# Separate logit products for the last batch's strided heads, ahead of its row products

## The chip, the cores and the metric

The kernel runs on one core of one Trainium2 chip. The metric is the device time of one execution in microseconds. Of the kernel before, three runs took 647.68, 648.56 and 649.07 us; their median is 648.56 us.

## The reference

Three stages follow each other. Attention has 4 batches, 8 heads, 576 positions and 64 features per head. Heads 0 to 3 ("local", kind 0) look at the last 32 positions, heads 4 to 7 ("strided", kind 1) at positions with the same remainder modulo 32. Its output, 2304 tokens by 512 features, goes to a mixture of 8 experts of which each token takes one, and then to a dense layer that takes the maximum of three products:

```
x = attn(q, k, v) -> (2304, 512)             # 4 local and 4 strided heads side by side
logits = (x / (|x| + 1e-6)) @ en.T / tau     # en: the 8 expert vectors, normalised
expert = argmax(logits); gate = softmax(logits)[expert]
y[t]   = gate[t] * (relu(x[t] @ w1[expert]) @ w2[expert])
out    = max(y @ w1', y @ w2', y @ w3') @ w_out
```

Token t is position t % 576 of batch t // 576. The kernel counts 18 tiles of 128 tokens; the last batch is given tiles 13 to 17, and tile 13 holds 64 tokens of batch 2 and 64 of batch 3.

## The kernel before, in words

The kernel writes its instructions in the order in which each engine is to carry them out; nothing reorders them later. So what stands behind an instruction on its engine waits when that instruction waits.

**Attention (attention, L696).** 44 groups of score blocks (11 a batch) go through a pipeline over the step number s: scores, maximum, exponential, norm, transposes, product with the values. The last of these, g_av (L421), copies its product with ScalarE into xT (L444), the attention output with features on partitions, 64 features of each of 2 heads on 128 partitions, two such halves c for each kind.

**Rows (tok_half, L458).** For tile i and one kind, two products (four for a tile with two batches) with xT as the weights and rhs_i as the moving operand turn the 128 tokens into rows. rhs_i has 136 columns: 128 of the identity, and 8 with the normalised expert vectors, so each row comes out with 128 features and 8 partial logits. A copy (ScalarE once the pipeline drains, L477) brings them from PSUM into rows; after kind 1, the row goes out to x_scr in HBM by a DMA on SyncE's queue (L482). The products' PSUM tiles have two buffers (ps_r).

**Routing of the last batch (route_stages(3), L491).** Its stages are carried out in this order (L648): logits, order, five squares, norm, gate, gate2. 
- logits (L508, VectorE): sums the four partial logits of each token (L511), then five short operations to the one-hot of the largest (L513 to L517).
- order (L585): TensorE counts the tokens of each expert (L590, L592), ranks the batch's tokens (rank, L525), adds up the token lists of tiles 0 to 12 (windows, L597 to L603) and runs a product that nobody reads (warm(WM), L604); VectorE works out slots and one-hots (L609 to L625, with the expert order eid_i at L624); windows of tiles 13 to 17 (L628); then the token lists win_i (L634 to L638).
- square (L502, ScalarE): the sum of squares of one tile's rows, both kinds.
- norm (L519, GpSimd): the root of the five sums by a power (L521), and an addition (L522). gate and gate2 make the softmax's weight from it.

**The first expert.** After the attention, gather(0) (L779, L997) fetches the first expert's rows from x_scr in three pieces by indirect DMAs, issued by GpSimd and addressed by win_i. SyncE loads the first weights (L130), after it has read eid_i (L626); from the third load on they stand behind a small GpSimd operation that waits for the last piece (L125). TensorE runs 6 products that nobody reads (L1005), then transposes the first two pieces (L815), runs 4 more such products (L813), transposes the third, and after a split by ScalarE and VectorE (L797, L798) the expert's products begin (L822); these fill TensorE from there on.

An example of the order that matters here: `return [(0, f) for f in (logits, order)] + sq + [(0, f) for f in (norm, gate, gate2)]` (L648) puts the squares behind everything that logits and order give to ScalarE, and the norm ahead of gather(0) on GpSimd.

Of the kernel before, what the change touches and what calls it, by code (L numbers as in the profile page):

```python
# [9 lines left out]
F32 = mybir.dt.float32  # L10
# [5 lines left out]
ALU = mybir.AluOpType  # L16
AX = mybir.AxisListType
PSUM = bass.MemoryType.PSUM

B, H, S, D = 4, 8, 576, 64  # L20
NT, DM, E, F, F2 = 2304, 512, 8, 1024, 768
# [18 lines left out]
AGF = 500  # L40
NCF = 2
MID = 0
WM = 1
WN = 6
WX = 4
NOW0 = 7000
# [22 lines left out]
def kernel(ctx, tc, a, out, x_scr, w_scr, u_scr, perm_scr, gate_scr, upto="all"):  # L69
    nc = tc.nc  # L70
# [215 lines left out]
    ps_s = actx.enter_context(tc.tile_pool(name="ps_s", bufs=PSS, space=PSUM))  # L286
    ps_t = actx.enter_context(tc.tile_pool(name="ps_t", bufs=PST, space=PSUM))
    ps_x = actx.enter_context(tc.tile_pool(name="ps_x", bufs=PSX, space=PSUM))
    ps_r = actx.enter_context(tc.tile_pool(name="ps_r", bufs=8 - PSS - PST - PSX, space=PSUM))
# [20 lines left out]
    rhs_i = pa.tile([128, 4, 136], F32, name="rhs_i")  # L310
    junk = pa.tile([128, 512], F32, name="junk")

    vv, xT = {}, {}
# [42 lines left out]
    later, later_v = [], []  # L356

    def flush(fs):
        while fs:
            fs.pop(0)()  # L360
# [89 lines left out]
    first_tile = {0: 0, 1: 4, 2: 9, 3: 13}  # L450
    n_tiles = {0: 4, 1: 5, 2: 4, 3: 5}
    rows = {}
# [2 lines left out]
    def bc(ap, shape):  # L455
        return ap.to_broadcast(shape)

    def tok_half(i, kind):  # L458
        ps = ps_r.tile([128, 512], F32, tag="r", name="r")
        psv = ps[:, 0:272].rearrange("p (c n) -> p c n", c=2)  # L460
        segs, done = [], 0
        while done < 128:
            b, off = divmod(128 * i + done, S)
            n = min(128 - done, S - off)
            segs.append((done, b, off, n))
            done += n
        for c in range(2):
            for p0, b, off, n in segs:
                nc.tensor.matmul(  # L469
                    out=psv[p0:p0 + n, c, :], lhsT=xT[b, kind][:, c, off:off + n],  # L470
                    rhs=rhs_i[:, 2 * kind + c, :], start=True, stop=True)
        bq = max(b for b in range(B) if i >= first_tile[b])
        if bq not in rows:
            rows[bq] = row_p.tile([128, 5, 4, 136], F32, tag="row", name="row")
        dst = rows[bq][:, i - first_tile[bq], 2 * kind:2 * kind + 2, :]
        if on_act[0]:
            later_v.append(lambda: nc.scalar.activation(out=dst, in_=psv, func=ACTF.Copy))  # L477
        else:
            later_v.append(lambda: nc.vector.tensor_copy(out=dst, in_=psv))
        if kind == 1:  # L480
            r = rows[bq][:, i - first_tile[bq], :, 0:128]
            later_v.append(lambda: nc.sync.dma_start(  # L482
                out=x_scr[128 * i:128 * i + 128, :].rearrange("n (c d) -> n c d", c=4), in_=r))

    def warm(n, what=cf, pool=None, tag="t"):

        ps = (pool or ps_t).tile([128, 512], F32, tag=tag, name="warm")
        for _ in range(n):
            nc.tensor.matmul(out=ps[:, 0:256], lhsT=what[:, 0:128], rhs=what[:, 0:256], start=True, stop=True)

    def route_stages(b):  # L491
# [4 lines left out]
        def small(nm, dt=F32):  # L496
            return sm_p.tile([128, 5, 1], dt, tag=nm, name=nm)[:, 0:T, :]

        def wide(nm, n=E, dt=F32):
            return sm_p.tile([128, 5, n], dt, tag=nm, name=nm)[:, 0:T, :]  # L500
# [7 lines left out]
        def logits():  # L508

            d["l"], d["mx"], v, vm = wide("l"), small("mx"), wide("v"), small("vm")  # L510
            nc.vector.tensor_reduce(  # L511
                out=d["l"], in_=rows[b][:, 0:T, :, 128:136].rearrange("p t c e -> p t e c"), axis=AX.X, op=ALU.add)
            nc.vector.tensor_reduce(out=d["mx"][:, :, 0], in_=d["l"], axis=AX.X, op=ALU.max)  # L513
            nc.vector.tensor_tensor(out=v, in0=d["l"], in1=bc(d["mx"], s8), op=ALU.is_ge)
            nc.vector.tensor_tensor(out=v, in0=v, in1=bc(edesc.unsqueeze(1), s8), op=ALU.mult)
            nc.vector.tensor_reduce(out=vm[:, :, 0], in_=v, axis=AX.X, op=ALU.max)
            nc.vector.tensor_tensor(out=oh_all[:, t0:t0 + T, :], in0=v, in1=bc(vm, s8), op=ALU.is_equal)  # L517
# [67 lines left out]
        def order():  # L585


            oh, ee = oh_all[:, t0:t0 + T, :], [128, E, E]
            ps = ps_s.tile([128, 512], F32, tag="s", name="cnt")[:, 0:E]
            nc.tensor.matmul(out=ps, lhsT=ones, rhs=coh, start=True, stop=False)  # L590
            for t in range(T):
                nc.tensor.matmul(out=ps, lhsT=ones, rhs=oh[:, t, :], start=False, stop=t == T - 1)  # L592
            rank()

            tb = ps_t.tile([128, 512], F32, tag="t", name="tb")[:, 0:NW]

            def windows(t):  # L597
                for u in range(2):
                    nc.tensor.matmul(
                        out=tb, lhsT=lo_oh[:, t, :], rhs=w_tok[:, t, u, :], start=t == u == 0, stop=t == NTILE - 1 and u == 1)  # L600

            for t in range(t0):
                windows(t)  # L603
            warm(WM)  # L604
            key, pos = (sm_p.tile([128, E], F32, tag=n, name=n) for n in ("key", "pos"))
            tmp = sm_p.tile(ee, F32, tag="tmp", name="tmp")
            sl, lo, w = wide("sl"), small("lo", I32), small("w", I32)
            z = z_all[:, t0:t0 + T]
            nc.vector.scalar_tensor_tensor(out=key, in0=ps, scalar=8.0, in1=edesc, op0=ALU.mult, op1=ALU.add)  # L609
            nc.vector.tensor_tensor(out=sl, in0=d["rkv"], in1=bc(ebase.unsqueeze(1), s8), op=ALU.add)  # L610
            nc.vector.tensor_tensor(out=cmp, in0=bc(key.unsqueeze(1), ee), in1=bc(key.unsqueeze(2), ee), op=ALU.is_gt)
            nc.vector.tensor_tensor(out=sl, in0=sl, in1=oh, op=ALU.mult)
            nc.vector.tensor_reduce(out=pos, in_=cmp, axis=AX.X, op=ALU.add)
            with nc.allow_low_precision(reason="whole numbers below 2**15"):
                nc.vector.tensor_reduce(out=z, in_=sl, axis=AX.X, op=ALU.add)
            nc.vector.tensor_tensor(
                out=posoh, in0=bc(pos.unsqueeze(1), ee), in1=bc(iota[:, 0:E].unsqueeze(2), ee), op=ALU.is_equal)
            nc.vector.tensor_scalar(out=lo[:, :, 0], in0=z, scalar1=127, scalar2=None, op0=ALU.bitwise_and)
            nc.vector.tensor_scalar(out=w[:, :, 0], in0=z, scalar1=7, scalar2=None, op0=ALU.arith_shift_right)
            nc.vector.tensor_tensor(out=tmp, in0=posoh, in1=bc(iota[:, 0:E].unsqueeze(1), ee), op=ALU.mult)  # L620
            d["lo"], d["w"] = lo, w
            onehots()
            with nc.allow_low_precision(reason="whole numbers below 8"):
                nc.vector.tensor_reduce(out=eid_i, in_=tmp, axis=AX.X, op=ALU.add)  # L624
            tokens()  # L625
            ev[0] = nc.sync.value_load(eid_i[0:1, 0:1], min_val=0, max_val=E - 1)  # L626
            w_load()
            for t in range(t0, NTILE):  # L628
                windows(t)

            for q0, q1 in ((0, 1), (1, E)):
                w4 = [128, q1 - q0, NWIN, E]
                wp = sm_p.tile(w4, F32, tag=f"wp{q0}", name="wp", bufs=1)
                nc.vector.tensor_tensor(  # L634
                    out=wp, in0=bc(tb.rearrange("p (e i) -> p i e", e=E).unsqueeze(1), w4),
                    in1=bc(posoh[:, q0:q1].unsqueeze(2), w4), op=ALU.mult)
                with nc.allow_low_precision(reason="whole numbers below 2**12"):
                    nc.vector.tensor_reduce(  # L638
                        out=win_i[:, NWIN * q0:NWIN * q1].rearrange("p (q i) -> p q i", i=NWIN), in_=wp, axis=AX.X, op=ALU.add)
            nc.vector.tensor_copy(out=cnt_f, in_=ps)  # L640
# [48 lines left out]
    def embed3():  # L689
# [3 lines left out]
        nc.vector.tensor_copy(out=rhs_i[:, :, 128:136], in_=ep[:, 0:32].rearrange("p (c e) -> p c e", e=8))  # L693
        nc.vector.tensor_copy(out=rhs_i[:, :, 0:128], in_=bc(ident.unsqueeze(1), [128, 4, 128]))

    def attention():  # L696
        loads = [(b, kind) for b in range(B) for kind in range(2)][1:]
        toks, todo = [], []
        last = [0]
        for s in range(NG + LA + 1):  # L700
# [17 lines left out]
            if 0 <= s - LA < NG:  # L718
                g_av(s - LA)
                b, k = divmod(s - LA, 11)  # L720
                if k in (4, 10):
                    ts = range(first_tile[b], first_tile[b] + n_tiles[b])
                    toks += [lambda: None] * (DT if s < NG - 6 else 0) + [lambda i=i, k=k: tok_half(i, k // 6) for i in ts]
                if k == 10:
                    toks.append(lambda b=b: todo.extend(route_stages(b)))
                if s >= NG:
                    flush(later)
# [652 lines left out]
```

## Time and profile before

| | |
|---|---|
| median of 3 runs | 648.56 us |
| profiled execution | 645.76 us |
| its span, first to last instruction | 644.0 us |
| TensorE busy | 612.5 us, 95% of the span |
| VectorE busy | 448.6 us, 70% |
| ScalarE busy | 337.4 us, 52% |
| GpSimd busy | 134.8 us, 21% |
| mean granted TensorE clock | 0.983 of full |

The profile is that of one execution; its times are microseconds from the span's start. PE is TensorE's matrix products, PEld its weight loads, DVE VectorE, ACT ScalarE, POOL GpSimd and SP SyncE (SPq is its queue). A float32 product stands as two records, with a weight load each. A busy TensorE is not one at its best, since the ends of products are modelled.

### The profile page before, as it was taken

The page shows a single profiled execution, that of the slowest core. Times are in us where ns is not written, and L with a number is a line of the kernel's source. Part 1 is how long each engine was busy: PE and PEld are TensorE (multiplying, and loading weights), DVE is VectorE, ACT ScalarE, POOL GpSimd, SP SyncE. Part 2 cuts the span into 40 slices and gives each one's busy share as a digit, 9 for nine tenths or more (in the row PEclk, how much of TensorE's full clock was granted, in tenths as well). Part 3 has the DMA queues.
Part 4 walks back from the last instruction along what each step waited for, and adds up shares of the span by engine and source line. Part 5 has one row for each costly group of instructions (what it writes and reads, how often), then busy time and mean ns, then how long its engine had stood idle before and what let it go on. Part 6 is the DMA issues. An engine that isn't in the chain of part 4 may idle for free.

```text
span 644.0 us, 11933 instructions
## 1 busy us (share of the span) xinstructions
PE 612.5 (95%) x4281; PEld 576.7 (90%) x4282; DVE 448.6 (70%) x1011; ACT 337.4 (52%) x909; POOL 134.8 (21%) x131
## 2 busy tenths in 40 slices
PE   7899998799989999999999799999999999999995
PEld 6788886599979999999999699988999988999984
DVE  6878988577689788978897788787344376335440
ACT  3678877455566666656664534536412246221242
POOL 5434433354313142322210000002100012000021
PEclk8999999799989999999999999999999999999998
DMA  8998761674879596876864778921177301367111
GB/s 234 295 247 216 220 177 52 194 241 165 276 255 337 191 325 238 295 292 210 285 234 148 275 286 321 345 96 66 59 268 268 125 17 66 133 250 264 57 49 53
DMA packets 44881, 130.81 MB, mean 203 GB/s; under 512 B 4633, under 2 KB 15513, under 8 KB 41457
## 3 DMA queue, kind: packets, MB, share of 16 engines
q1 hardware_dynamic: 41792, 120.50, 56.3%
q0 software_dynamic: 3024, 9.49, 4.0%
q8 instruction: 36, 0.59, 0.4%
q14 instruction: 29, 0.23, 0.1%
HBM read 97.73 MB, written 32.24 MB: 202 GB/s over the span
## 4 chain that ended last, share of the span: by engine, by line
PE 80%; DVE 8%; DMA 8%; issue 1%; ACT 1%; SPq 1%; POOL 0%; POOLq 0%; DVEq 0%; ACTq 0%
PE g L822 61%; PE q L822 10%; DMA qs<-qs 2%; PE s L376 2%; PE x L434 2%; PE r L469 2%; PE q L805 1%; DMA ks<-kts 1%; DMA stage<-w_scr 1%; DMA out<-r,perm_i 1%; PE t L415 1%; DMA em<-emb 1%; DVE pt L417 1%; DVE mx L383 1%; DVE w L171 1%
## 5 line engine op out<-in xcount | busy, mean ns | idle before, releaser
L822 PE MATMUL g<-xc,w 128*128 128x384 f32 x1134 | 200.3, 336 | 4.8 <-DVE hf L1105 3.8
L822 PEld LDWEIGHTS g<-xc,w 128*128 128x128 f32 x1134 | 197.8, 189 | 7.0 <-issue 4.1
L171 DVE TENSOR_TENSOR w<-stage,w 128x1024 fp32r<-128x1024 f32 x76 | 105.9, 1405 | 26.4 <-ACT w L166 25.0
L822 PE MATMUL g<-h,w 128*128 128x376 f32 (+7 forms) x768 | 112.8, 303 | 2.2 <-DVE h L842 2.2
L822 PEld LDWEIGHTS g<-h,w 128*128 128x128 f32 x768 | 105.6, 190 | 3.5 <-DVE h L842 2.9
L822 PE MATMUL g<-xw,w 128*128 128x376 f32 (+7 forms) x768 | 106.0, 298 | 0.5 <-ACT xw L797 0.3
L822 PEld LDWEIGHTS g<-xw,w 128*128 128x128 f32 x768 | 104.3, 189 | 0.9 <-ACT xw L797 0.6
L166 ACT ACTIVATE w<-stage 128x1024 fp32r<-128x1024 f32 x76 | 79.3, 1056 | 16.1 <-DMA stage<-w 15.4
L1171 POOL DMA_INDIRECT out<-r,perm_i x18 | 17.8, 991 | 284.4 <-ACT r L1170 202.0
L822 PE MATMUL q<-w,hs 128*128 128x512 f32 x324 | 74.9, 390 | 1.3 <-DVE hs L1159 1.3
L822 PEld LDWEIGHTS q<-w,hs 128*128 128x128 f32 x324 | 60.6, 188 | 14.8 <-DVE hs L1159 2.6
L395 ACT ACTIVATE p<-s,nb 128x96 f32<-128x96 f32 (+2 forms) x152 | 50.6, 346 | 21.5 <-DVE r L404 16.0
L239 POOL TENSOR_TENSOR f<-f,c 128x512 int32<-128x512 int32 x24 | 31.4, 1307 | 117.1 <-DVE f L237 80.1
L1107 DVE TENSOR_TENSOR tmp<-g,yt 128x384 f32<-128x384 f32 x36 | 20.0, 555 | 44.6 <-PE g L822 44.4
L1120 ACT ACTIVATE yt<-g 128x384 f32<-128x384 f32 x27 | 13.3, 491 | 71.0 <-PE g L822 50.9
L407 POOL TENSOR_TENSOR p<-p,ri 128x384 f32<-128x384 f32 (+3 forms) x44 | 35.9, 816 | 59.2 <-DVE ri L406 45.2
L841 ACT ACTIVATE h<-g 128x376 fp32r<-128x376 f32 (+7 forms) x64 | 25.8, 410 | 29.8 <-PE g L822 27.9
L960 DVE TENSOR_TENSOR xc<-yt,xc 128x384 fp32r<-128x384 f32 x42 | 21.4, 553 | 15.7 <-ACT xc L959 15.7
L856 ACT ACTIVATE yt<-g 128x376 f32<-128x376 f32 (+7 forms) x32 | 13.2, 413 | 36.1 <-PE g L822 35.1
L417 DVE COPY pt<-t 96x512 f32<-96x512 f32 (+3 forms) x44 | 25.5, 581 | 8.0 <-PE t L415 7.8
L786 POOL DMA_INDIRECT xg<-x_scr,win_i x22 | 26.1, 1186 | 23.3 <-PE q L936 10.2
L395 ACT ACTIVATION_READ_ACCUMULATOR p<-s,nb 128x1 f32 (+2 forms) x152 | 31.0, 204 | 0.0
(175 smaller groups left out, 789.1 us busy)
## 6 DMA issues: line engine op xcount, KB each, us to landing
stage<-w SPq DMA_DIRECT2D x64, 512.0 KB
c<-wm SPq DMA_DIRECT2D x24, 512.0 KB
w<-u_scr SPq DMA_DIRECT2D x12, 1024.0 KB
u_scr<-w SPq DMA_DIRECT2D x9, 1024.0 KB
w<-u_scr SPq DMA_DIRECT2D x12, 768.0 KB
u_scr<-w SPq DMA_DIRECT2D x9, 768.0 KB
w_scr<-f SPq DMA_DIRECT2D x24, 256.0 KB
stage<-w_scr SPq DMA_DIRECT2D x12, 512.0 KB
```

The source lines that it names most:

```text
L166: nc.scalar.activation(out=ws[i][:, 0, 0:m], in_=x, func=ACTF.Copy)
L171: nc.vector.tensor_tensor(out=ws[i][:, 1, 0:m], in0=x, in1=ws[i][:, 0, 0:m].bitcast(F32), op=ALU.subtract)
L239: nc.gpsimd.tensor_tensor(out=f, in0=f, in1=low, op=ALU.add)
L395: nc.scalar.activation(out=p[:nq, i, :nk], in_=st[g]["ps"][:nq, i * nk:(i + 1) * nk], func=ACTF.Exp, bias=st[g]["nb"][:nq, i:i + 1], scale ...
L407: nc.gpsimd.tensor_tensor(out=d["p"][:nq, 0:ns, :nk], in0=d["p"][:nq, 0:ns, :nk], in1=ri[:nq, 0:ns].to_broadcast([nq, ns, nk]), op=ALU.mult)
L417: nc.vector.tensor_copy(out=pts[:nk, 0:ns, :nq], in_=pt[:nk, 0:ns * nq].rearrange("p (s q) -> p s q", s=ns))
L786: nc.gpsimd.indirect_dma_start(out=t[i][:r], out_offset=None, in_=x_scr, in_offset=bass.IndirectOffsetOnAxis(ap=win_i[:r, NWIN * e + i:NWI ...
L822: nc.tensor.matmul(out=ps, lhsT=ws(i), rhs=xs(j), start=first and n == 0, stop=last and n == 2, skip_group_check=more)
L841: nc.scalar.activation(out=h[:, 0], in_=ps, func=ACTF.Relu)
L960: nc.vector.tensor_tensor(out=x[:, 1], in0=src[c], in1=x[:, 0].bitcast(F32), op=ALU.subtract)
L1107: nc.vector.tensor_tensor(out=tmps[i], in0=ps, in1=s, op=ALU.add)
L1171: nc.gpsimd.indirect_dma_start(out=out, out_offset=bass.IndirectOffsetOnAxis(ap=perm_i[:, col:col + 1], axis=0), in_=r, in_offset=None)
```

## The change

The last batch's partial logits of the strided heads no longer come from the rows. A new function multiplies xT of kind 1 with the 8 expert columns alone, for all five tiles, into one PSUM tile. VectorE sums the two partial logits of the local heads from the rows and adds that PSUM tile. The row products of kind 1 come behind: three tiles (LR) in logits, two in order, behind the windows of tiles 0 to 12, where warm(WM) stood. The routing stages themselves keep their order.

```
+    def logit_products():
+        ps_l.append(ps_s.tile([128, 512], F32, tag="s", name="lg")[:, 0:40].rearrange("p (t e) -> p t e", e=E))
+        for t in range(n_tiles[B - 1]):
+            for p0, b, off, n in segments(first_tile[B - 1] + t):
+                for c in range(2):
+                    nc.tensor.matmul(
+                        out=ps_l[0][p0:p0 + n, t, :], lhsT=xT[b, 1][:, c, off:off + n], rhs=rhs_i[:, 2 + c, 128:136],
+                        start=c == 0, stop=c == 1, skip_group_check=True)
...
         def logits():
             d["l"], d["mx"], v, vm = wide("l"), small("mx"), wide("v"), small("vm")
+            m = 2 if b == B - 1 else 4
             nc.vector.tensor_reduce(
-                out=d["l"], in_=rows[b][:, 0:T, :, 128:136].rearrange("p t c e -> p t e c"), axis=AX.X, op=ALU.add)
+                out=d["l"], in_=rows[b][:, 0:T, 0:m, 128:136].rearrange("p t c e -> p t e c"), axis=AX.X, op=ALU.add)
+            if b == B - 1:
+                nc.vector.tensor_tensor(out=d["l"], in0=ps_l[0], in1=d["l"], op=ALU.add)
+                some_tiles(LR)
...
             for t in range(t0):
                 windows(t)
-            warm(WM)
+            some_tiles(n_tiles[b])
...
+    def some_tiles(n):
+        while n and later_tiles:
+            tok_half(later_tiles.pop(0), 1)
+            flush(later_v)
+            n -= 1
...
-                if k in (4, 10):
+                if k == 10 and b == B - 1:
+                    toks += [lambda: logit_products(), lambda: flush_todo(todo), last_route]
+                    later_tiles.extend(range(first_tile[b], first_tile[b] + n_tiles[b]))
+                elif k in (4, 10):
```

flush(later_v) carries out the ScalarE copy of the tile and the DMA to x_scr at that place; last_route carries out all stages of route_stages(3) one after the other.

## Rows read from the trace of the kernel before

**Rows 1.** The page: span, TensorE's busy time, the chain's shares by engine.

```profile
span 644.0 us, 11933 instructions
...
PE 80%; DVE 8%; DMA 8%; issue 1%; ACT 1%; SPq 1%; POOL 0%; POOLq 0%; DVEq 0%; ACTq 0%
```

**Rows 2.** The chain, 103 to 131 us: start, us, engine, what, line.

```profile
111.45 0.42 ACT xt L444
...
111.92 3.13 PE r L469 x22
...
115.06 0.41 ACT row L477
...
115.50 0.45 DVE l L511
...
117.15 0.29 PE cnt L592 x5
...
120.31 0.43 PE tb L599 x10
...
121.75 4.54 DMA xg<-x_scr,win_i
...
126.42 1.22 PE g L815 x8
127.64 1.73 PE warm L489 x8
...
130.70 0.44 PE g L822
```

**Rows 3.** Timeline of GpSimd, 119 to 125 us; in brackets idle time before, and releaser.

```profile
119.17 1.38 POOL L521 TENSOR_TENSOR nrm<-ssq,ca 128x5 f32<-128x5 f32 x1 [9.16 <-ACT junk L505]
120.64 0.24 POOL L522 TENSOR_SCALAR nr<-nrm 128x5 f32<-128x5 f32 x1
121.75 1.23 POOL L786 DMA_INDIRECT xg<-x_scr,win_i  x1 [0.86 <-DVE wp L634]
123.28 0.96 POOL L786 DMA_INDIRECT xg<-x_scr,win_i  x1 [0.31 <-issue]
```

**Rows 4.** Timeline of ScalarE: the first of the five squares, and the last one's end.

```profile
115.36 0.62 ACT L505 ACTIVATE junk<-row 128x512 f32<-128x512 f32 x1
...
118.90 0.19 ACT L505 ACTIVATION_READ_ACCUMULATOR junk<-row 128x1 f32 x1
```

**Rows 5.** Timeline of TensorE: weight loads (PEld) and products of three kinds.

```profile
105.70 0.41 PEld L415 LDWEIGHTS t<-cf,p 126*126 126x126 f32 x4 [0.17 <-issue]
...
111.91 0.42 PEld L469 LDWEIGHTS r<-rhs_i,xt 128*64 128x64 f32 x6 [0.54 <-ACT xt L444]
...
112.52 2.30 PEld L469 LDWEIGHTS r<-rhs_i,xt 128*128 128x128 f32 x16 [0.18 <-issue]
...
117.46 0.85 PE L599 MATMUL tb<-w_tok,lo_oh 128*128 128x24 bf16 x26
```

**Rows 6.** Timeline of VectorE: the last operation of batch 2's routing.

```profile
113.53 0.17 DVE L581 TENSOR_TENSOR coh<-coh,ohs 128x8 bf16<-128x8 bf16 x1
```

**Rows 7.** Timeline of SyncE: the last batch's five stores.

```profile
113.05 3.41 SPq L482 DMA_DIRECT2D x_scr<-row  x5
```

**Rows 8.** Stretches: length, busy us and instructions by engine, granted clock (1.00 full), DMA share, GB/s.

```profile
116.00:117.00 1.00, 0.00 (x0) 0.00 (x0) 0.86 (x5) 0.94 (x4) 0.00 (x0) 1.00 1.03 288
...
118.00:119.00 1.00, 1.00 (x14) 0.63 (x10) 1.00 (x8) 0.97 (x4) 0.00 (x0) 0.50 0.68 193
...
123.00:124.00 1.00, 1.00 (x4) 0.82 (x3) 0.17 (x1) 0.00 (x0) 0.72 (x1) 0.52 1.03 422
...
127.00:128.00 1.00, 1.00 (x8) 0.95 (x8) 0.95 (x1) 0.00 (x0) 0.00 (x0) 1.00 0.40 160
```

**Rows 9.** Timeline of TensorE: unread products, and the second piece's transposes' loads.

```profile
120.58 4.50 PE L489 MATMUL warm<-cf 128*128 128x256 f32 x12
...
126.98 0.42 PEld L815 LDWEIGHTS g<-cf,xg 128*128 128x128 f32 x4 [0.17 <-DMA xg<-x_scr,win_i]
```

More of the change, by code (lines that the diff above doesn't have):

```diff
@@ L42 @@
 MID = 0
-WM = 1
+LR = 3
 WN = 6
@@ L456, in bc, with segments @@
         return ap.to_broadcast(shape)
-    def tok_half(i, kind):
-        ps = ps_r.tile([128, 512], F32, tag="r", name="r")
-        psv = ps[:, 0:272].rearrange("p (c n) -> p c n", c=2)
+    def segments(i):
         segs, done = [], 0
@@ L466, in tok_half @@
             done += n
+        return segs
+    ps_l = []
+    def logit_products():
[6 more added lines that the diff above has]
+                        start=c == 0, stop=c == 1, skip_group_check=True)
+    def tok_half(i, kind):
+        ps = ps_r.tile([128, 512], F32, tag="r", name="r")
+        psv = ps[:, 0:272].rearrange("p (c n) -> p c n", c=2)
+        segs = segments(i)
         for c in range(2):
@@ L694, in embed3, with flush_todo, last_route @@
         nc.vector.tensor_copy(out=rhs_i[:, :, 0:128], in_=bc(ident.unsqueeze(1), [128, 4, 128]))
+    later_tiles = []
+    def flush_todo(todo):
+        while todo:
+            todo.pop(0)[1]()
+    def last_route():
+        for _, f in route_stages(B - 1):
+            f()
+    def some_tiles(n):
[3 more added lines that the diff above has]
+            n -= 1
     def attention():
@@ L720, in attention @@
                 b, k = divmod(s - LA, 11)
-                if k in (4, 10):
+                if k == 10 and b == B - 1:
+                    toks += [lambda: logit_products(), lambda: flush_todo(todo), last_route]
+                    later_tiles.extend(range(first_tile[b], first_tile[b] + n_tiles[b]))
+                elif k in (4, 10):
                     ts = range(first_tile[b], first_tile[b] + n_tiles[b])
                     toks += [lambda: None] * (DT if s < NG - 6 else 0) + [lambda i=i, k=k: tok_half(i, k // 6) for i in ts]
-                if k == 10:
+                if k == 10 and b < B - 1:
                     toks.append(lambda b=b: todo.extend(route_stages(b)))
```

## The prediction, made before the changed kernel was run

> **What bounds the kernel now.** The page comes first: TensorE holds 80% of the chain that ended last, and the profiled execution's span is 644.0 us [rows 1]. The rest of the chain matters where TensorE has nothing to do, so I read next the chain around the end of the attention, where the change lies. There the reader sees a relay: the last copy of xT, 22 product records for the strided rows, the last row copy, the logits, the counts, the last windows, then the gather of the first expert's rows at 121.75, its landing, the transposes, eight records of unread products, and the expert's products from 130.70 [rows 2]. Behind 130.70 TensorE runs nearly without a gap, so a microsecond at the first gather or at the transposes is a microsecond of the whole.
>
> The chain names one releaser for each step. So the third view is GpSimd's own timeline: the gather stands there behind the norm, which began at 119.17, when ScalarE's last square had ended, and with its addition ended at 120.88; the gather follows at 121.75 with 0.86 of idle time [rows 3]. The norm is late by less than a microsecond of being what holds the gather. This side branch (row copies, squares, norm, gather) is not in the chain, and it is what the change touches.
>
> **The change part by part.** Times below are on the profiled execution's clock.
>
> *The products.* They replace nothing; the 24 records (12 products) are added. Four belong to batch 2's half of tile 13 and can run before xT is ready. Of the 20 others, four load 64 columns and 16 load 128, and each moves only 8 columns. No such product stands in the trace. Below: 26 bf16 products with 24 columns took 0.85, 0.033 each; above: the rows' own records took 3.13 for 22, 0.142 each [rows 2, 5]. I take the weight loads as the limit, since these shrink with nothing: 0.41 for four of 126 columns, so 0.103, and 0.42 for six of 64, so 0.07 [rows 5]. That is 16 x 0.103 + 4 x 0.07 = 1.93 from 111.92, plus some 0.15 until the last result is there: 114.0 (112.7 to 114.9 by the ends).
>
> *The logits.* VectorE has batch 2's routing until 113.70 [rows 6], so cheap products would not be used sooner anyway. The sum over the local halves reads half of what L511 read in 0.45; about 0.3, until 114.0. The added operation and the five that follow cost what the five cost now: from 115.50 + 0.45 to 117.15 is 1.2, 0.24 each [rows 2]. One-hots at 114.05 + 0.24 + 1.2 = 115.5, where they now come at 117.1.
>
> *Three row tiles ahead of the counts.* These are 8 + 4 + 4 = 16 records on TensorE, 16 x 0.142 = 2.3 from about 113.85, so 116.1 (115.0 if they run at 0.07 and 0.103). The counts stand behind them: 116.1 instead of 117.15, a gain of 1.05, and not the 1.6 that the one-hots gain. The two VectorE chains from the counts to win_i are unchanged, so win_i would be ready 1.05 earlier, and the gather could leave at 120.7.
>
> *Two row tiles behind the windows.* On TensorE they take the place of unread products and end before the one-hots for the last windows are there, so they cost TensorE nothing. But all that a tile issues moves with it: its ScalarE copy and its store. The counts, the rank and the windows took 117.15 to about 118.15; so the two tiles begin at 117.1, need 8 x 0.142 = 1.14, and the last copy (0.41) ends at 118.7. Now it ends at 115.47 [rows 2]. **This is the price.** The five squares stand behind that copy on ScalarE: they took from 115.36 to 119.09 [rows 4], and the norm began 3.70 behind the last copy's end. It will begin at 122.4 and, with the same 1.71 to the end of the addition, end at 124.1. The gather stands behind it on GpSimd. With the 0.05 to 0.31 that separate waiting GpSimd operations [rows 3], it leaves at about 124.25 instead of 121.75: **+2.5**. Its bounds: with every TensorE record at its cheapest and the one-hots at 115.3, the last copy still ends at 117.5, which makes +1.35; with products at 0.142 and the clock halved while tiles 16 and 17 run, it ends near 120.2, which makes +4.0. That win_i is earlier is lost behind this.
>
> *SyncE's queue.* The two late stores stand there ahead of the reading of the first expert's number and the weight loads. Five stores took 3.41 to issue [rows 7], so two take 1.4, until about 119.9. The weights are not in the chain between the gather and 130.70 [rows 2], and they stay out of it when the gather is later. Costed at nothing; if they were late, it could be at most the 1 us or so by which their loads slip. gate and gate2 wait for the norm on VectorE, with weight splits behind them; these too have until the third transposes.
>
> *The clock.* The granted clock fell to half when TensorE had nothing to do from about 115.0 to 117.15, and came back at 123.96, during the 12 unread products that began at 120.58 [rows 8, 9]. That left the transposes and the products at full clock. After the change TensorE is busy from 111.9 to 118.3, ends the 12 products sooner (at 0.216 each, as the eight took 1.73, they are through near 121.7), and then has nothing to do until the first piece lands near 128: 6 us, three times the idle stretch after which the clock fell. I expect half clock for the transposes and the eight unread products. The price by rows: the clock stayed at half for 3.4 us of work, 120.58 to 123.96, in which half of that, 1.7, was lost; there it was hidden, here it is in the chain. **+1.7**. Bounds: nothing if the clock stays, 2.9 if the eight products (+1.73), eight transposes (twice 0.42 for each four, +0.8) and the first expert products all run at half.
>
> *Behind 130.* The second piece, not the first, starts the transposes that the unread products follow [rows 9], so a quicker landing of the first piece gains nothing.
>
> The sum: 2.5 + 1.7 = +4.2. Against the profiled execution, 645.76 (span 644.0 and 1.76 around it), that is 650.0. The three runs lie 1.9 to 3.3 above that execution; I add the difference to their median: 648.56 + 4.2 = **652.8**.
>
> **The rivals.**
>
> *A. Later gather, clock kept* (+2.5, 651.1). For it: before, an idle stretch of 1.3 between the 12 products and the transposes did not bring the clock down. Against: the new one is over four times as long.
>
> *B. The norm doesn't hold, the stores do* (no change). If squares and norm came out early, the gather would still wait for the rows of tiles 16 and 17 in x_scr. The five stores, 1.28 MB, moved until about 118.7, 3.2 behind the last copy [rows 2, 8]. From a last copy at 118.2 to 118.7 the landing is at 121.4 to 121.9, against a gather at 121.75 now: -0.35 to +0.15, 648.2 to 648.7. The Trainium skill (DMA: Bandwidth & Descriptors, Anatomy of one DMA) puts the fixed cost of a transfer at about 2.0 us, most of it the receipt of the write, beside its bytes at 436 GB/s; by that, as an estimate, the last store would land at 121.3 to 121.8, and the 3.2 of the trace agrees, as there the stores stood in line.
>
> *C. Faster: win_i decides.* It ends on the other side if neither branch holds the gather: one-hots 1.6 earlier, gather 1.05 to 1.5 earlier, 647.1 to 647.5. For it: the chain puts the gather down to VectorE, not to the norm [rows 3]. It decides at one point: the last copy would have to end at 115.4 or before, since norm's end has only 0.86 to give. By TensorE's order the copy is behind the counts, and these behind the one-hots, so it can't.
>
> *D. Heavier* (+6.5, 655.1): the norm at its upper bound, +4.0, and the clock at 2.5.
>
> **How the numbers follow.** Forecast 0.51, A 0.21, D 0.08, B 0.10, C 0.10. The forecast's own range is 650.5 to 655. The range reaches from 648.2 (B's lower end) to 655.8 (between D and its bounds), leaving out C, a little of B and of D. About 0.2%, 1.3 us, is what a measurement of this kernel tells from no change: slower by more takes the forecast, A and D, 0.80, less 0.02 for A's low end: 0.78; within 0.2%: B, that end, and 0.02 of C that stays under 1.3: 0.14; faster: 0.08.
>
> **What would show each step.** In the changed kernel's GpSimd timeline the norm should begin near 122.4 and the gather near 124.25 with next to no idle time ahead of it, or with idle time ended by something of the norm's line; the chain should run through the squares or the norm. The last row copy should end near 118.7 and the counts begin near 116.1. The 20 product records should take about 1.9; 0.7 would show that weight loads are hidden. The granted clock should be half around 128 to 131. I am wrong if the gather leaves before 122.5, if it is released by win_i or the stores, or if TensorE's first expert product starts before 132.

## The result and the profile after

The kernel became slower. In four runs each, the changed kernel's median is 656.65 us (655.23 to 658.42) and that of the kernel before 648.82 us (647.68 to 649.65): the medians differ by 7.8 us, and the ratio is 1.0127 with a 95% interval of 1.0086 to 1.0167, or 8.2 us (5.6 to 10.8). The profiled execution took 655.23 us.

First the page of the changed kernel: span and the chain's shares, which answer to [rows 1].

```profile
span 653.4 us, 11979 instructions
...
PE 78%; DVE 8%; DMA 8%; ACT 2%; issue 2%; POOL 1%; SPq 0%; POOLq 0%; DVEq 0%; ACTq 0%
```

TensorE lost two points of the chain, ScalarE and GpSimd gained them: a side branch has come onto the path. Which one, the chain of waits of the changed kernel shows, 114 to 140 us (start, us, engine, what, line), against [rows 2].

```profile
114.41 2.28 PE lg L475 x20
116.69 2.38 PE r L485 x16
119.08 0.13 PE cnt L612 x5
...
120.09 1.67 PE r L485 x8
121.78 0.40 ACT row L493
122.18 0.62 ACT junk L521 x2
...
125.89 1.20 POOL nrm L541
...
128.28 1.23 POOL xg L825
...
129.82 3.81 DMA xg<-x_scr,win_i
133.68 1.11 PE g L854 x4
134.79 3.41 PE warm L505 x8
...
139.62 0.44 PE g L861
```

Before, the chain left the rows at the logits and went through counts and windows to the gather. Now it goes through the two late row tiles, their last copy, the five squares and the norm. Since the last xT copy ended 2.49 us later in this execution, ahead of anything that the change touches, I count from T0, the start of the first product behind that copy: 111.92 before, 114.41 after. GpSimd's timeline of the changed kernel, to hold against [rows 3]:

```profile
125.89 1.20 POOL L541 TENSOR_TENSOR nrm<-ssq,ca 128x5 f32<-128x5 f32 x1 [13.38 <-ACT junk L521]
127.17 0.24 POOL L542 TENSOR_SCALAR nr<-nrm 128x5 f32<-128x5 f32 x1
128.28 1.23 POOL L825 DMA_INDIRECT xg<-x_scr,win_i  x1 [0.86 <-DVE df L585]
129.82 1.44 POOL L825 DMA_INDIRECT xg<-x_scr,win_i  x1 [0.31 <-issue]
```

The gather left 13.87 behind T0, before 9.83: +4.04. The 0.86 idle ahead of it is the 0.86 of before. The releaser in the bracket (df, which ends at 127.95) has nothing that the gather reads.

Stretches of 1 us of the changed kernel (busy time by engine, third from the end the granted clock), to hold against [rows 8]:

```profile
117.00:118.00 1.00, 1.00 (x11) 0.78 (x8) 0.86 (x5) 0.40 (x1) 0.00 (x0) 0.92 0.00 0
118.00:119.00 1.00, 1.00 (x8) 0.93 (x9) 0.09 (x1) 0.40 (x1) 0.00 (x0) 0.50 0.03 8
...
128.00:129.00 1.00, 0.00 (x0) 0.00 (x0) 0.56 (x3) 1.00 (x2) 0.72 (x1) 0.54 0.72 295
135.00:136.00 1.00, 1.00 (x4) 0.81 (x3) 0.00 (x0) 0.00 (x0) 0.20 (x1) 0.50 0.00 0
```

The clock fell twice. The second fall, at 128, follows an idle stretch, as forecast. The first, just before 118, came with TensorE busy the whole microsecond before it. TensorE's timeline shows what each cost.

```profile
119.94 1.81 PE L485 MATMUL r<-rhs_i,xt 128*128 128x136 f32 x8
...
122.35 2.84 PE L505 MATMUL warm<-cf 128*128 128x256 f32 x12
132.07 1.09 PE L854 MATMUL g<-cf,xg 128*128 128x128 f32 x4 [6.88 <-DMA xg<-x_scr,win_i]
133.68 1.11 PE L854 MATMUL g<-cf,xg 128*128 128x128 f32 x4 [0.52 <-DMA xg<-x_scr,win_i]
134.58 3.62 PE L505 MATMUL warm<-cf 128*128 128x256 f32 x8
...
139.04 3.25 PE L861 MATMUL g<-xw,w 128*128 128x376 f32 x15 [0.30 <-ACT xw L836]
```

In the chain the eight unread products took 3.41 against 1.73 before [rows 2], and the first product of the expert came at 139.04, 24.63 behind T0. In the trace of before it stands at 130.11 (18.19 behind T0), so the stage is 6.44 longer. From there to the end of the span both need the same: 644.0 - 130.11 = 513.9, and 653.4 - 139.04 = 514.4.

### The profile page after: what moved, and what is told of

It is laid out like the page before. It is cut to its first block, busy times and chain, and to the rows that moved or that the text cites. A ratio compares the mean times of both kernels' runs of the same rounds, so it can differ in the third digit from the quotient of the medians.

```text
span 653.4 us, 11979 instructions
## 1 busy us (share of the span) xinstructions
PE 617.3 (94%) x4303; PEld 581.6 (89%) x4304; DVE 448.6 (69%) x1012; ACT 337.4 (52%) x909; POOL 135.5 (21%) x131
## 4 chain that ended last, share of the span: by engine, by line
PE 78%; DVE 8%; DMA 8%; ACT 2%; issue 2%; POOL 1%; SPq 0%; POOLq 0%; DVEq 0%; ACTq 0%
PE g L861 57%; PE q L861 11%; PE s L376 3%; DMA qs<-qs 2%; DMA stage<-w 2%; PE r L485 2%; PE x L434 2%; DMA ql<-ql 1%; PE t L415 1%; DMA stage<-w_scr 1%; PE q L844 1%; DVE w L171 1%; DVE pt L417 1%; DVE mx L383 1%; DMA xg<-x_scr,win_i 1%
## 5 line engine op out<-in xcount | busy, mean ns | idle before, releaser
L239 POOL TENSOR_TENSOR f<-f,c 128x512 int32<-128x512 int32 x24 | 33.1, 1379 | 115.5 <-DVE f L237 95.5
L825 POOL DMA_INDIRECT xg<-x_scr,win_i x22 | 25.4, 1153 | 24.8 <-PE q L975 10.8
```

The source lines that it names most:

```text
L239: nc.gpsimd.tensor_tensor(out=f, in0=f, in1=low, op=ALU.add)
L825: nc.gpsimd.indirect_dma_start(out=t[i][:r], out_offset=None, in_=x_scr, in_offset=bass.IndirectOffsetOnAxis(ap=win_i[:r, NWIN * e + i:NWI ...
```

## The experiments

The theory: the gather is held by the norm, the norm by the squares, these by the late row copies; half clock makes the row products and the transposes slow. Rivals: the stores hold the gather, win_i holds it, or the added products alone cost the time. No kernel leaves work out; where products are added or widened, the added results are not read. The table has distances from T0 in one profiled execution of each, and the ratio of runs to the kernel before on the same chip.

| kernel | last row copy ends | gather leaves | first expert product | ratio [95%] |
|---|---|---|---|---|
| before | +3.54 | +9.83 | +18.19 | |
| after | +7.77 | +13.87 | +24.63 | 1.0127 [1.0086, 1.0167] |
| e1_gather_first | +9.22 | +13.24 | +23.36 | 1.0076 [1.0046, 1.0105] |
| e2_squares_early | +8.42 | +12.61 | +23.28 | 1.0106 [1.0079, 1.0133] |
| e3_clock_held | +9.24 | +15.33 | +24.20 | 1.0083 [1.0047, 1.0120] |
| e4_before_gather_first | +3.55 | +9.50 | +18.29 | 1.0001 [0.9975, 1.0028] |
| e5_wide_products | +6.76 | +12.86 | +23.31 | 1.0114 [1.0076, 1.0152] |
| e6_all_tiles_ahead | +6.66 | +12.75 | +22.45 | 1.0135 [1.0095, 1.0175] |
| e7_repaired | +6.76 | +10.77 | +19.80 | 1.0041 [1.0020, 1.0063] |
| e8_products_alone | +7.00 | +13.24 | +21.63 | 1.0102 [1.0068, 1.0135] |
| e9_before_clock_held | +3.55 | +9.80 | +18.79 | 1.0014 [0.9988, 1.0040] |
| e10_wide_and_held | +6.77 | +12.87 | +22.22 | 1.0059 [1.0031, 1.0087] |
| e11_wide_products_alone | +6.02 | +12.26 | +20.81 | 1.0052 [1.0029, 1.0075] |
| e12_rows_ahead_of_windows | +6.11 | +10.75 | +19.25 | 1.0031 [1.0003, 1.0060] |

The interval of each edit that repairs one thing in the changed kernel (e1, e2, e3, e5, e6) meets the changed kernel's own, so the runs don't price these parts; their prices below are read from one profiled execution each. Of its repaired forms only e7 and e12 are clear of it in the runs.

**e1_gather_first**: the first gather stands ahead of the squares and the norm.

```
-        return [(0, f) for f in (logits, order)] + sq + [(0, f) for f in (norm, gate, gate2)]
+        return [(0, f) for f in (logits, order, gather0)] + sq + [(0, f) for f in (norm, gate, gate2)]
...
-    gather(0)
+    xg[0] = xg0
```

> The changed kernel with the first expert's gather issued on GpSimd ahead of the norm (squares and norm come behind it). Theory (queue): in the changed kernel the gather is held by the norm, the norm by the five squares, these by the last row copy. Then the gather leaves once win_i and the stores are there, 3.2 to 4.8 us sooner than now: in the changed kernel win_i was written at 122.93 and the stores moved data until about 124.6, and the gather left at 128.28. First expert product 3 to 7 us sooner (7 if the shorter idle time of TensorE also keeps the clock), time 650 to 653.5. Rival (stores): the late stores of tiles 16 and 17 hold the gather; then nothing is gained, 656 to 657. Rival (elsewhere, attention or weight loads): the gather leaves sooner, but the time stays at 656 to 657.

Measured: the copy ended 1.45 later than in the changed kernel, since the clock fell earlier still (the 20 product records took 3.31 instead of 2.28), and yet the gather left 0.63 earlier, where 3.2 to 4.8 were expected. GpSimd's timeline and the chain of this kernel:

```profile
128.46 1.24 POOL L676 DMA_INDIRECT xg<-x_scr,win_i  x1 [15.15 <-issue]
```
```profile
124.04 0.40 ACT row L493
...
124.61 2.80 DMA x_scr<-row
127.41 0.03 POOLq L676
...
127.61 0.85 issue
```

From the last copy's end to the gather it is 4.02, where it was 6.10 with the norm between. So the norm did hold the gather, by 2.1 (e7 and e10 below differ by as much with the clock full in both), and what holds it next is the stores, not win_i.

**e2_squares_early**: the norm stays ahead, but three of the five squares go right behind the first three tiles.

```
+                for t in range(LR):
+                    square(t)
...
-        return [(0, f) for f in (logits, order)] + sq + [(0, f) for f in (norm, gate, gate2)]
+        return [(0, f) for f in (logits, order)] + sq[LR:] + [(0, f) for f in (norm, gate, gate2)]
```

> The changed kernel with the squares of the first three row tiles given to ScalarE straight behind their copies, ahead of the counts, so that two squares and not five stand behind the last copy. Queue theory: the norm begins 3 x 0.75 = 2.2 us sooner, the gather as much, time about 654.4, lower by up to 2 more if the clock is kept. Rival (stores, or win_i, hold the gather): the norm begins 2.2 us sooner, the gather does not, 656 to 657.

Measured: copy to gather 4.19, and the idle time between the norm's addition and the gather rose from 0.86 to 1.22, so the norm was no longer what held it:

```profile
125.22 1.23 POOL L827 DMA_INDIRECT xg<-x_scr,win_i  x1 [1.22 <-DVE smx L594]
```

The releaser in the bracket (smx) has nothing that the gather reads, and the chain doesn't name the stores here. That they held the gather is inferred: it left 3.8 behind the issue of the last store, as in e1 and e7 (3.8 to 3.9), where the chain does name them.

**e3_clock_held**: 22 unread products instead of 6 while TensorE waits for the gather.

```
-WN = 6
+WN = 22
```

> The changed kernel with 22 unread products (44 records) instead of 6 ahead of the transposes, 9.5 us at 0.216 each, to fill TensorE's idle stretch before the gather's landing. If the clock's fall costs what I read from the trace (5.94 us from the second piece's transposes to the first expert product, 3.72 before the change), that stretch goes back to about 3.7 and the time to about 654.4. If the clock isn't the cause of these 2.2 us: no change, 656 to 657. If the products overrun the landing, some of the gain is lost, up to 1 us.

TensorE's timeline of this kernel:

```profile
133.49 0.66 PE L854 MATMUL g<-cf,xg 128*128 128x128 f32 x4 [1.36 <-DMA xg<-x_scr,win_i]
133.98 1.89 PE L505 MATMUL warm<-cf 128*128 128x256 f32 x8
135.71 0.58 PE L854 MATMUL g<-cf,xg 120*128 120x120 f32 x4
136.61 1.71 PE L861 MATMUL g<-xw,w 128*128 128x376 f32 x6 [0.33 <-ACT xw L836]
```

From the second transposes to the first expert product it is 3.12, against 5.36 in the changed kernel and 3.13 before (the 5.94 and 3.72 expected from are counted to the product behind VectorE's xw, 139.62 and 130.70). So the second fall of the clock costs 2.2. The gather itself left 1.46 later (the first fall came earlier here, as in e1), which ate most of that in this profile.

**e4_before_gather_first**: the edit of e1 made in the kernel before, to see whether its norm held the gather.

```
-        return [(0, f) for f in (logits, order)] + sq + [(0, f) for f in (norm, gate, gate2)]
+        return [(0, f) for f in (logits, order, gather0)] + sq + [(0, f) for f in (norm, gate, gate2)]
...
-    gather(0)
+    xg[0] = xg0
```

> The kernel before with the first expert's gather issued ahead of the norm. It tells what held the gather there. The idle time between the norm's addition and the gather was 0.87 before and 0.86 after the change, though win_i was ready at very different distances; so I now think that the norm held it in both. Then the gather leaves some 0.3 to 0.5 us sooner, when win_i is there (written at 121.17), and the time is 0 to 0.7 us lower, 648.1 to 648.8. If win_i held it (as the chain of waits has it): the gather leaves at the same distance from win_i, 0.58, and nothing changes.

The chain of this kernel, around the gather and the expert's start:

```profile
121.23 0.18 DVE win_i L638
...
121.71 1.24 POOL xg L656
...
131.24 0.47 DVE xw L809
...
131.75 4.36 PE g L833 x24
```

The gather left 0.30 behind win_i instead of 0.86 behind the norm, 0.33 earlier from T0. The norm had held it in the kernel before too, by that third of a microsecond. The runs gained nothing: the gate now comes late, the weight split behind it also, and the expert's product waits for VectorE's xw.

**e5_wide_products**: the added products move 102 columns instead of 8.

```
-        ps_l.append(ps_s.tile([128, 512], F32, tag="s", name="lg")[:, 0:40].rearrange("p (t e) -> p t e", e=E))
+        ps_l.append(ps_s.tile([128, 512], F32, tag="s", name="lg")[:, 0:510].rearrange("p (t e) -> p t e", e=102))
...
-                        out=ps_l[0][p0:p0 + n, t, :], lhsT=xT[b, 1][:, c, off:off + n], rhs=rhs_i[:, 2 + c, 128:136],
+                        out=ps_l[0][p0:p0 + n, t, :], lhsT=xT[b, 1][:, c, off:off + n], rhs=rhs_i[:, 2 + c, 34:136],
...
-                nc.vector.tensor_tensor(out=d["l"], in0=ps_l[0], in1=d["l"], op=ALU.add)
+                nc.vector.tensor_tensor(out=d["l"], in0=ps_l[0][:, :, 94:102], in1=d["l"], op=ALU.add)
```

> The changed kernel with the separate products 102 columns wide instead of 8 (94 columns that nobody reads; the same weight loads). In the changed kernel the granted clock fell at 117.9, 3.5 us after the products had begun and with TensorE never idle since; in three later traces of its variants it fell during or right behind them. Theory (the narrow products let the clock fall): with wide ones the 20 records take no longer (2.2 to 2.4 us, since the weight loads set their pace), the clock stays at full through the row products, and the last row copy ends 6.8 us behind the first product instead of 7.8 (9.2 in the worst trace so far); gather 1 us sooner or more, time 1 to 2 us lower, 654.6 to 655.6. Rival (the clock falls for another reason, such as the idle stretches around the xT copies): no change in clock or time. Rival (columns set the pace): the 20 records take 0.5 us longer or more.

Stretches of this kernel, columns as above:

```profile
117.00:118.00 1.00, 1.00 (x18) 1.00 (x15) 1.00 (x8) 0.14 (x1) 0.00 (x0) 1.00 1.02 288
118.00:119.00 1.00, 0.29 (x3) 0.18 (x2) 0.97 (x4) 0.93 (x3) 0.00 (x0) 1.00 1.05 308
...
127.00:128.00 1.00, 0.00 (x0) 0.00 (x0) 0.96 (x2) 0.08 (x1) 0.91 (x1) 0.64 0.53 197
```

The 20 records took 2.52 instead of 2.28, and the clock stayed at full through the row products; it fell only in the later idle stretch. The last copy ended at +6.76: 1.0 earlier than with 8 columns, although the products are wider. So the first fall of the clock costs 1.0 at the copy and as much at the gather in the profile of the changed kernel; where it came earlier (e1, e3) the copy ended 2.5 later than here.

**e6_all_tiles_ahead**: all five row tiles ahead of the counts.

```
-LR = 3
+LR = 5
```

> The changed kernel with all five row tiles of kind 1 ahead of the counts, none behind the windows. Theory (the two tiles behind the windows make the last row copy late): the counts come 1.2 us later, but the last copy ends about 6.4 us behind the first product instead of 7.8, so norm and gather come 1.4 us sooner, time about 655.2. If win_i held the gather: 1.2 us later, 657.8.

Measured: copy and gather 1.1 earlier than in the changed kernel and the first expert product 2.2 earlier, but the runs are where the changed kernel's are. The interval of the ratio spans 5 us, so this neither shows a gain nor rules out one of 2 us.

**e7_repaired**: gather first (e1), wide products (e5) and more unread products together. To e1's edit and e5's comes:

```
-WN = 6
+WN = 16
```

> The changed kernel with three repairs: gather ahead of the norm, products 102 columns wide, and 16 unread products (32 records, 6.9 us) to hold the clock until the gather lands. The theory has these terms of the loss: gather held by the norm 2.0, clock in the row products 1.0, clock at transposes and after 2.2; together 5.2 of some 6.4 to 7.8. What remains is the late landing of the stores, 4.0 us behind the last row copy (6.8 + 4.0 = 10.8 from the first product to the gather, against 9.8 before the change), so 1 us or a little more: 649.9 to 651.5. If a cause outside these three carries the loss, the time stays above 653.

TensorE's timeline of this kernel, from the added products on:

```profile
113.74 2.52 PE L475 MATMUL lg<-rhs_i,xt 128*64 128x102 f32 x20 [0.17 <-ACT xt L444]
116.19 1.91 PE L485 MATMUL r<-rhs_i,xt 128*64 128x136 f32 x16
...
118.90 1.17 PE L485 MATMUL r<-rhs_i,xt 128*128 128x136 f32 x8
...
130.91 1.89 PE L505 MATMUL warm<-cf 128*128 128x256 f32 x8
...
134.55 1.63 PE L872 MATMUL g<-xw,w 128*128 128x376 f32 x8 [0.57 <-DVE xw L848]
```

The clock was full throughout: tiles 16 and 17 took 1.17 instead of 1.81, the eight unread products 1.89 instead of 3.62. The gather left at +10.77, the first expert product came at +19.80, and the loss fell from 8.2 us (5.6 to 10.8) to 2.7 (1.3 to 4.1, by the ratio); the intervals don't meet. So the three causes, repaired together, make up some two thirds of the loss. What is left in the stage: the gather 0.9 later than before, held by the stores, and then VectorE's xw, 0.57.

**e8_products_alone** and **e11_wide_products_alone**: the kernel before, with nothing but the added products put ahead of its row products, their results unread; 8 columns in e8, and in e11 102.

```
+    def unread_products():
+        ps = ps_s.tile([128, 512], F32, tag="s", name="lg")[:, 0:40].rearrange("p (t e) -> p t e", e=E)
...
+                    nc.tensor.matmul(
+                        out=ps[done:done + n, t, :], lhsT=xT[b, 1][:, c, off:off + n], rhs=rhs_i[:, 2 + c, 128:136],
+                        start=c == 0, stop=c == 1, skip_group_check=True)
...
+                if k == 10 and b == B - 1:
+                    toks.append(unread_products)
```

(e11: `[:, 0:510]`, `e=102` and `34:136` in place of `[:, 0:40]`, `e=E` and `128:136`.)

> The kernel before with the separate products added at the same place and their result unread; row products, logits and everything else as before. This prices the added part by itself: 2.2 us on the way to the row copies, the logits and the gather, at full clock; if the narrow products also let the clock fall, the 22 row records take up to 2 us longer and the time is 2.2 to 4.5 us above the kernel before, 651 to 653.5. If the products hide beside other work: no change, 648.9.

> The kernel before with the unread separate products, now 102 columns wide. Theory (the products cost 2.2 to 2.5 us of TensorE, and the rest of what the narrow ones cost, 6.9 us above before with an interval of 4.4 to 8.7, is the clock): 2.5 us above the kernel before, with an interval that reaches to 1.5 and 4. Rival (the products cost 5 us or more for another reason): as much above before as the narrow ones.

The same stretch of e8, and then of e11:

```profile
117.00:118.00 1.00, 1.00 (x9) 0.80 (x6) 0.00 (x0) 0.40 (x1) 0.00 (x0) 0.58 0.00 0
```
```profile
117.00:118.00 1.00, 1.00 (x8) 0.84 (x7) 0.00 (x0) 0.58 (x3) 0.00 (x0) 1.00 0.00 0
```

By the ratios e11 lost 3.4 us (1.9 to 4.9; the medians differ by 2.6), within which the 2.52 of its products lie; its copy ended 2.48 later than before and its gather left 2.43 later. In e8 the clock fell, the copy ended 3.46 later, and the runs lost 6.6 (4.4 to 8.7), though its stage grew by only 3.4 in the profile. The fall of the clock therefore doesn't come from the new order of the row products: the 8-column products bring it by themselves. And the added products alone, at full clock, cost about their own length, before any row tile is moved.

**e9_before_clock_held**: the kernel before with unread products in its idle stretch and behind it.

```
-WN = 6
+WN = 12
...
+            warm(4, cf, ps_x, "x")
```

> The kernel before with its clock held in the same stretch: 4 unread products (8 records, 1.7 us) in TensorE's idle time between the row products and the counts, and 12 instead of 6 ahead of the transposes (24 records, 5.2 us). In the profiled execution of before the clock fell at 117.1 and was back at 123.96, in time for the transposes; but runs of that kernel spread from 644 to 652 us and the slower ones show a lower mean clock. Theory (where the clock comes back too late, the transposes and the first expert products run at half): the clock stays full from 112 to 131, and the median falls by 1 to 2 us against the kernel before. Rival (before loses nothing here, since its 12 records always bring the clock back in time): no change, or 0.3 us slower where the added products meet the transposes.

Measured: no gain, but the clock was not held either. It still fell at about 121.6, ahead of the unread products:

```profile
121.00:122.00 1.00, 0.07 (x3) 0.16 (x4) 0.84 (x4) 0.00 (x0) 1.00 (x1) 0.81 0.00 0
```

The 24 records of these then ran past the landing of the first piece (first expert product +18.79 instead of +18.19). So the gather's place gains nothing in the kernel without the change (e4), while this run doesn't show what a held clock would give there; that all that e7 regained is the change's own cost is likely, and not shown.

**e10_wide_and_held**: e5 with more unread products; the norm stays ahead of the gather.

```
-WN = 6
+WN = 20
```

> The changed kernel with products 102 columns wide and 20 unread products to hold the clock, but with the gather behind the norm as in the change. Against the repaired kernel (which also has the gather first) it prices the order on GpSimd by itself. Theory: last row copy 6.8 us behind the first product, gather 12.9, first expert product 21.2 (18.2 before the change), so 3.0 us above the kernel before, and 1.4 to 2.1 above the repaired one. Rival (the order on GpSimd is worth nothing once the clock is held): the same time as the repaired kernel, within 0.5 us.

Measured: full clock throughout, the gather at +12.87 as expected, the first expert product at +22.22, 1.0 later than expected. From e7 it differs by GpSimd's order: 2.1 at the gather and 2.4 at the product. From e5 it differs by the clock behind the gather: from gather to product 9.35 instead of 10.45, although the second and third gather took 1.93 and 1.97 to issue.

**e12_rows_ahead_of_windows**: e7, with the two late row tiles ahead of the windows instead of behind them.

```
+            some_tiles(n_tiles[b])
             for t in range(t0):
                 windows(t)
-            some_tiles(n_tiles[b])
```

> The repaired kernel (gather first, wide products, clock held) with the two late row tiles ahead of the windows of tiles 0 to 12 instead of behind them. If the stores of the last rows hold its gather (4.0 us behind the last row copy, 2.5 behind win_i), the last copy ends 0.7 us sooner, the gather leaves 0.7 us sooner, and win_i, ready 2.5 us ahead of the gather, is not missed though it comes up to 0.4 later; time 0.7 us lower than the repaired kernel, some 2 to 2.5 above before. If something else holds the gather: unchanged.

The chains of e7 and of e12 between the last copy and the gather:

```profile
120.11 0.40 ACT row L493
...
120.67 2.79 DMA x_scr<-row
...
124.51 1.24 POOL xg L676
```
```profile
119.39 0.40 ACT row L493
...
119.96 3.42 DMA x_scr<-row
...
124.42 1.24 POOL xg L676
```

The copy ended 0.65 earlier, but the gather left no earlier. The last store only took its place in line: the five stores together moved at some 290 GB/s without a gap until 123 in both. By these two traces the gather waits for the bytes of all five, from the first store on, and not for the last copy. None of the kernels beat the kernel before.

## Why the prediction was right or wrong

The direction and the path were right; the size was too small. I gave 652.8 us and a range up to 655.8; the median was 656.65. On the profile's own clock the sum was +4.2 and the stage grew by 6.4.

*The products*: 2.28 measured from T0, 2.08 forecast. Weight loads set their time, as assumed: they are busy for 2.19 of the 2.28, and 94 more columns cost 0.24 (e5). What I didn't see is what they did to the clock, below.

*The counts*: 4.53 behind T0 against 5.23 before, forecast 4.2. Nothing came of it, since win_i (written at 122.9) was ready 5.3 ahead of the gather. Rival C fell.

*The late row tiles*: **the failed step.** The last copy was to end at +6.78 and ended at +7.77. I had the clock at half while tiles 16 and 17 run as an upper bound only, taking it that the clock falls when TensorE is idle, as in [rows 8]. It fell with TensorE busy. In the kernels with wide products and the same order, where it didn't fall, the copy ended at +6.76 and +6.77 (e5, e10), so the rest of the sum came out right. That is in part luck: the wide products took 0.44 longer than forecast, and the three tiles, counts and windows behind them 0.46 less (2.64 in e7, from 2.52 to 5.16 behind T0, against 3.10).

*Copy to norm*: 3.71 against the 3.70 of [rows 2 to 4]; norm and addition 1.52, not 1.71.

*Norm to gather*: **the second miss.** I took 0.05 to 0.31 (0.09 and 0.31 stand between operations in [rows 3]) and it was 0.86, the same idle time as in [rows 3]. I had read the 0.86 there as slack, because the row named VectorE as releaser. e4 shows that there was 0.3 of slack in the other direction: without the norm the gather leaves earlier.

At the gather these make 0.99 + 0.71 - 0.19, so 4.0 where I had 2.5. That is the upper bound I gave, reached by another sum than I had for it.

*The clock behind the gather*: forecast +1.7, measured +2.4, of which 2.2 is the half clock (e3 takes it away) and 0.2 stands ahead of the second transposes, whose gather took 1.44 to issue instead of 0.96. I priced it by one stretch of 3.4 us of work; the second transposes to the first expert product alone are 5.36.

*SyncE's queue*: the stores took 5.07 to issue instead of 3.41 and the first weight loads stand at 124.47; they are not in the chain. Costed at nothing, rightly.

*The rivals.* A (the clock stays) fell. B (the stores hold) is wrong for this kernel but right for what comes next: with the norm out of the way they hold (e1, e7 and e12 by the chain, e2 by inference). B's estimate takes from the Trainium skill (DMA: Bandwidth & Descriptors, Anatomy of one DMA) a fixed cost that the page gives for transfers issued from GpSimd; these stores are SyncE's, and in e1 they landed 2.5 to 2.8 us behind their issue. D (+6.5) is what happened, to 0.1 in the profile, with luck in its first half, which was reached by another sum; I had given it 0.08. Each of its two halves had a row against my middle value: the 0.86 of idle time, and 6 us of idle TensorE.

*What stays open.* The medians differ by 7.8, the stage by 6.4 and what follows it by 0.5. The other 0.9 lies inside the interval of the ratio, and no profile of one execution can place it. One candidate is the moment of the first fall: in e1 and e3 it came earlier, and the copy ended at +9.2, 1.5 later than in the profile of the changed kernel. The same holds for e6 and e8, whose runs and profiled stages differ by more (e6: stage +4.3, runs +8.7 by the ratio; e8: +3.4, +6.6).

## What to carry to other kernels

Work that is put ahead of a critical chain costs its own length first; here that was 2.3 to 2.5 us against a gain of 0.7 at the counts, and the rows that paid for it fed a second branch (copy, squares, norm) that looked as if it had 0.86 us of slack and had none (e4). Before trusting such slack, list everything queued ahead of the last instruction on its engine and what that waits for: an idle time that ends with the same length in every kernel is not slack. And where a trace shows TensorE's clock falling in an idle stretch, price the work behind a longer one at half clock; but don't take idleness for the only thing that brings it down, as here narrow products did.

## What the runs showed of the hardware

*A busy TensorE at half clock.* In all six traces with the 8-column products the granted clock fell 1.0 to 3.8 us behind T0, during these products or the row products behind them. In none of the five with 102 columns did it fall there, although the same weights are loaded in nearly the same time (2.28 and 2.52). The traces show that the narrow products bring the fall, not why.

*0.84 to 0.87 us ahead of the first gather.* From the end of the norm's addition to the first gather it was 0.86 or 0.87 wherever the norm stood ahead and nothing else held the gather. Without it the gather left 0.30 behind win_i (e4). But in e1, e7 and e12, where the stores came last and no computation stood ahead, the chain has 0.84 or 0.85 of issue just before the gather too. So the traces don't show that the computation brings this time.

*Gather issue beside VectorE's weight split.* The issue of the second or third gather piece took 0.95 to 0.99 where VectorE had no split (two inputs in SBUF), and mostly 1.27 to 2.05 where it started during one: 1.44 after, 1.80 and 1.27 in e3, 1.93 and 1.97 in e10. Two that began near a split's end and one that began at its start took no longer than usual. The Trainium skill (SBUF — State Buffer, Who interferes with whom) says that a VectorE instruction with two SBUF inputs contends with a GpSimd instruction that reads SBUF. The longer issues agree with it, if the issue of a gather reads its addresses (win_i) from SBUF. The same section reports a probe in which such an operation did not stall DMA, and infers that the making of descriptors needs the write side of the shared ports; these gathers, which have addresses to read, were longer beside one. No run here took the split away alone.
